# Filter spectrum stored on SP's queue from the first step of u on, two more input chunks in the positions' space, first spilled reads on SP

## The chip, the cores and the metric

One Trainium2 chip, one of its cores. The metric is the device time of one execution in microseconds (us); of several runs the median is given, and less is better.

## The reference, cut to what matters

```python
h_mlp = np.maximum(pos_emb @ w1, 0.0) @ w2          # [12480, 128], the filter
h_filt = h_mlp * np.exp(-0.01 * pos)[:, None]
u = x * v
y = irfft(rfft(u, 2 * S) * rfft(h_filt, 2 * S))[:S]  # causal long convolution
x1 = x * y
...
h = x1 @ w_in;  x2 = np.maximum(h, 0.0) ** 2 @ w_out              # first MLP, 128 -> 2048 -> 128
h = x2 @ w_in2; out = (h * sigmoid(1.702 * h)) @ w_out2           # second MLP
```

## The kernel before

The convolution is done as a two-step Fourier transform with 99 x 127 points, in matmuls. The program falls into these stages on the time line.

1. **Filter stage** (`filter_stage`). 16 transfers bring the positions' embeddings `pos`; matmuls, a relu and a window make `h`, 64 features, in SBUF. On the way the loads of the first chunks of `x` and `v` are issued.
2. **First transform of h.** 16 calls of `s1_step`, each 4 features: 8 matmuls (two records each in the trace) into a PSUM bank, then one copy on ACT into `G`, the filter's spectrum after the first step. Four PSUM banks rotate.
3. **First transform of u.** 32 calls of `s1_step`, each 4 of the 128 channels, into `A`. Their input is `u = x * v`, folded by VectorE (`Inputs.fold`: one multiplication, L206, then a sum, L207, and a difference, L208). `x` and `v` come in 16 chunks of 8 channels; a chunk feeds two steps. `Inputs.load` issues a chunk as four transfers on SP's queue: 96 rows of `x`, 96 rows of `v`, then the last 3 rows of each. `u` has 7 buffers.
4. **Second transform, product, first inverse** (`stage_s2`), with matrices `m` loaded on SP's queue and slices `Gs` of the filter's spectrum.
5. **Inverse and the two MLPs** (`mlp`).

`G` and `A` do not both fit for all of stage 4, so `G` is spilled: in stage 3 four transfers store it to `gd` in device memory (L637, ACT's queue, after steps 6, 10, 14 and 18 of u), and `load_h` reads it back in slices of 8 (`Gs`, L278, ACT's queue; the first two are issued after steps 26 and 28 of u).

Where chunks live: the first 5 have a buffer each beside `h` (pool `hp`). All others share 3 buffers in pool `vp`, so chunk 8 waits until chunk 5 is folded, chunk 9 until chunk 6 is folded, and so on. The code lines are

```python
c = self.loaded
if c == NXC or c >= self.early and c - max(self.done, self.early) == 3:
    return
```

`mh`, the pool of `w2b`, `m` and `Gs`, is opened after the last chunk's load is issued and lies where `vp` lay; a tile of it waits for the chunks whose bytes it takes. `A` lies where `hp` lay.

The order of the instructions on each engine is that of the code (`manual_schedule`). An engine's queue issues in order: a transfer that waits holds back what stands behind it, and on ACT's queue transfers stand between the copies. Each transfer signals its end on one of eight semaphores, which the built program hands out in turn over both queues; a transfer waits until the transfer before it on its semaphore has landed.

Of the kernel before, what the change touches and what calls it, by code (L numbers as in the profile page):

```python
# [23 lines left out]
N1, N2 = 99, 127  # L24
# [4 lines left out]
F = 64  # L29
# [5 lines left out]
NXC = D // XC  # L35
HK = 4
HL = 8
# [54 lines left out]
def conv_mlp_kernel(ctx: ExitStack, tc: tile.TileContext, xc, xt, vc, pt, w1, w2,  # L92
                    moe_w_in, moe_w_out, moe2_w_in, moe2_w_out,
                    c_s1, c_s2, c_i2, c_win, out):
    nc = tc.nc
# [8 lines left out]
    gd = dram.tile([128, N1, 2 * F], FP32, name="gd")  # L104
# [45 lines left out]
    def split_weights(pool, l):  # L150
        wr = pool.tile([128, 4 * DFF], FP32, name=f"w{l}").bitcast(F32R)
        wr = wr.rearrange("p (a b) -> p a b", a=4)
        wts.append(wr)

    class Weights:
# [3 lines left out]
        def __init__(self, chunks, start, gap, lead, pool, rest=()):  # L159
            self.pool, self.raw, self.run = pool, {}, []  # L160
            self.plan = [(int(start + k * gap), n) for k, n in enumerate(chunks)]
            self.fetches = [(at - lead, n) for at, n in self.plan] + [(at, n) for at, n in rest]
            self.plan += [(1 << 30, n) for at, n in rest]
# [15 lines left out]
    class Inputs:  # L179


        def __init__(self, up, pool, first, early):
            self.up, self.pool, self.tiles, self.u = up, pool, {}, {}
            self.first, self.early = first, early
            self.loaded = self.done = 0

        def load(self):
            c = self.loaded
            if c == NXC or c >= self.early and c - max(self.done, self.early) == 3:
                return  # L190
            self.loaded += 1
            pool, bufs = (self.first, self.early) if c < self.early else (self.pool, 3)
            xs, vs = (pool.tile([N1, XC, 2, NJ], FP32, tag=n, name=n, bufs=bufs) for n in ("x", "v"))
            for r in (slice(0, ROWS), slice(ROWS, N1)):
                nc.sync.dma_start(out=xs[r], in_=xc[c, r])
                nc.sync.dma_start(out=vs[r], in_=vc[c, r])
            self.tiles[c] = xs, vs
# [56 lines left out]
    def s1_step(bank, src, d, dst):  # L254


        ps = bank("s1").rearrange("p (e k) -> p e k", e=4)[:, :, 0:2 * N1]
        for e in range(4):
            for half in range(2):
                j = slice(half * NJ, (half + 1) * NJ)  # L260
                nc.tensor.matmul(out=ps[j, e], lhsT=src[:, d + e, j], rhs=cs1[:, half])  # L261
        nc.scalar.copy(out=dst, in_=ps.rearrange("p e (c k) -> p k c e", c=2))

    m_t, h_t = {}, {}

    def load_m(mp, p):
        if p >= NP:
            return
        n = min(2, N1 - 2 * p)
        m_t[p] = mp.tile([128, 2, 2, 128], FP32, tag="m", name="m", bufs=7)  # L270
        nc.sync.dma_start(out=m_t[p][:, 0:n], in_=c_s2[:, 2 * p:2 * p + n])

    def load_h(mp, g):
        if g >= NHL:
            return
        n = min(HL, N1 - g * HL)
        h_t[g] = mp.tile([128, HL, 2 * F], FP32, tag="Gs", name="Gs", bufs=2)
        nc.scalar.dma_start(out=h_t[g][:, 0:n], in_=gd[:, g * HL:g * HL + n])  # L278

    def stage_s2(sp, mp, A, w2b, hooks, work):  # L280

# [8 lines left out]
        with kp as kp, obp as obp:  # L290
# [57 lines left out]
            for p in range(NP + 2):  # L348
                if p < NP:
                    spectra(p)  # L350
                if p % 2 == 0:
                    features(p // 2 + 1)
                if 0 <= p - 2:
                    back(p - 2)
                load_m(mp, p + 5)
                if p % 4 == 1:
                    load_h(mp, p // 4 + 2)
                if 0 <= p - 1 < NP:
                    product(p - 1)
                work.tick(p)  # L360
                for f in hooks.get(p, ()):
                    f()
# [18 lines left out]
    def load_x(lp, t):  # L381
        x_t[t] = lp.tile([D, MW], FP32, tag="xs", name="xs", bufs=2)
        w = width(t)
        nc.sync.dma_start(out=x_t[t][:, 0:w], in_=xt[:, STARTS[t]:STARTS[t] + w])
# [214 lines left out]
    with tc.manual_schedule():  # L599
        ups, sgs, vps = ExitStack(), ExitStack(), ExitStack()  # L600
        up = ups.enter_context(tc.tile_pool(name="u", bufs=7, side="right", reuse_waits="tile"))
        cps = ups.enter_context(tc.tile_pool(name="bank", bufs=4, space=PSUM))

        def bank(name):
            return cps.tile([128, 1024], FP32, tag="b", name=name)

        G = sgs.enter_context(tc.tile_pool(name="G", bufs=1, side="right")).tile(
            [128, N1, 2, F], FP32, name="G")
        vp = vps.enter_context(tc.tile_pool(name="v", bufs=3, side="right"))
        folds = {max(-(-11 * c // 5) + 1, 2 * c + 4 if c >= 7 else 0) for c in range(NXC)}  # L610
        steps = [0]

        def advance():
            if steps[0] in folds:
                inputs.fold()
            inputs.load()
            steps[0] += 1

        with tc.tile_pool(name="h", bufs=1) as hp:
            h = hp.tile([N1, F, 2 * NJ], FP32, name="h")  # L620
            inputs = Inputs(up, vp, hp, 5)
            with tc.tile_pool(name="fil", bufs=2) as fp:
                filter_stage(fp, bank, h, inputs)
            for f in range(0, F, 4):
                s1_step(bank, h, f, G[:, :, :, f:f + 4])
                advance()
            assert inputs.done >= inputs.early
        with tc.tile_pool(name="A", bufs=1, reuse_waits="tile") as ap_, ExitStack() as mps:
            A = ap_.tile([128, N1, 2, D], FP32, name="A")
            for d in range(0, D, 4):  # L630
                s1_step(bank, inputs.u[d // XC], d % XC, A[:, :, :, d:d + 4])
                if d // 4 < 22:
                    advance()
                if d // 4 in (6, 10, 14, 18):
                    q = 25 * (d // 16 - 1)
                    q = slice(q, min(q + 25, N1))
                    nc.scalar.dma_start(out=gd[:, q], in_=G[:, q].rearrange("p k c f -> p k (c f)"))  # L637
                if d // 4 == 22:
                    assert inputs.done == NXC
                    vps.close()  # L640
                    mp = mps.enter_context(tc.tile_pool(name="mh", bufs=1, reuse_waits="tile"))
                    w2b = mp.tile([128, 2 * D], FP32, name="w2b")
                    nc.sync.dma_start(out=w2b, in_=w2)
                if 22 <= d // 4 < 27:
                    load_m(mp, d // 4 - 22)
                if d // 4 in (26, 28):
                    load_h(mp, (d // 4 - 26) // 2)
            sgs.close()
            ups.close()
            w0 = ctx.enter_context(tc.tile_pool(name="w0", bufs=1, side="right", reuse_waits="tile"))  # L650
            split_weights(w0, 0)
            cp = ctx.enter_context(tc.tile_pool(name="cvt", bufs=1, side="right", reuse_waits="tile"))
            lp = ctx.enter_context(tc.tile_pool(name="lp", bufs=2, side="right", reuse_waits="tile"))
            nc.sync.dma_start(out=ci2, in_=c_i2)
            work = Weights([0, 4, 1, 5, 2, 6], 3, 7, 5, cp, [(44, 3), (46, 7)])
            hooks = {44: [lambda: load_x(lp, 0)]}
            with tc.tile_pool(name="s2", bufs=1, side="right", reuse_waits="tile") as sp:
                stage_s2(sp, mp, A, w2b, hooks, work)
        w1_ = ctx.enter_context(tc.tile_pool(name="w1", bufs=1, side="right", reuse_waits="tile"))
        split_weights(w1_, 1)  # L660
        mlp(lp, cp)
# [89 lines left out]
```

## Time and profile before

| what | value |
|---|---|
| median of 3 runs | 1435.65 us (1435.14 to 1436.28) |
| profiled execution, its own time | 1431.45 us |
| its span, first to last instruction | 1429.7 us |
| mean granted TensorE clock in it | 0.992 |
| PE busy, share of the span | 98% |
| DVE, ACT, POOL busy | 78%, 66%, 16% |

A busy share is the time in which an engine had an instruction under way; a waiting PE shows as a gap, a throttled one as a granted clock under 1. The median is of runs without a profile.

### The profile page before, as it was taken

Reading aid. Unit: us, or ns where it says so; the run is one execution under the profiler, and the core shown is the slowest. Engines: PE = TensorE matmul, PEld = TensorE weight load, DVE = VectorE, ACT = ScalarE, POOL = GpSimd, SP = SyncE. Lnnn points to the kernel's source line nnn. Section 1 sums busy time; section 2 is a strip of 40 time slices with the busy share of each in tenths; the row PEclk is TensorE's granted clock in tenths of the full one; section 3 lists DMA queues with packets and bytes.
Section 4 is the critical chain, followed back from the end, with each engine's and each line's share of the span. In section 5 each row is a group of like instructions: output and inputs, shape, how many; then the busy total and the mean of one; then the engine's idle time right before and its main releaser. Section 6 shows DMA issues by size and latency. Waiting matters only on the chain.

```text
span 1429.7 us, 17766 instructions
## 1 busy us (share of the span) xinstructions
PE 1403.7 (98%) x7018; PEld 1177.1 (82%) x7018; DVE 1115.9 (78%) x1233; ACT 939.9 (66%) x1066; POOL 224.8 (16%) x209
## 2 busy tenths in 40 slices
PE   8989999999999999999999999999999999999998
PEld 7858888688878888888888888888888888888887
DVE  7348998699997777877778777877777777777887
ACT  2534454377767776776777777776777776777776
POOL 3002232317521110021101210112101120000000
PEclk9989999899999999999999999999999999999999
DMA  9586766411300001000001000010000000000000
GB/s 254 198 264 216 250 230 224 154 44 64 96 6 22 19 27 38 8 26 19 27 9 36 19 27 26 8 38 19 26 11 24 30 26 8 8 8 1 15 15 15
DMA packets 46400, 91.34 MB, mean 64 GB/s; under 512 B 4183, under 2 KB 30604, under 8 KB 45804
## 3 DMA queue, kind: packets, MB, share of 16 engines
q1 hardware_dynamic: 35886, 57.17, 13.8%
q10 hardware_dynamic: 10430, 33.03, 6.0%
q8 instruction: 55, 0.90, 0.3%
q14 instruction: 29, 0.24, 0.0%
HBM read 64.33 MB, written 25.85 MB: 63 GB/s over the span
## 4 chain that ended last, share of the span: by engine, by line
PE 92%; DVE 4%; DMA 3%; ACT 1%; issue 1%; SPq 0%; DVEq 0%; ACTq 0%
PE hin L484 12%; PE hin L483 12%; PE acc L484 12%; PE hin L485 12%; PE acc L483 12%; PE acc L485 12%; PE yps L441 4%; PE s L261 3%; PE hk L311 3%; PE xk L313 3%; PE ob L337 3%; PE fk L300 2%; DMA v<-in_vc_dram 1%; DVE gl L521 1%; DMA gd<-G 1%; DVE r L245 1%
## 5 line engine op out<-in xcount | busy, mean ns | idle before, releaser
L521 DVE TENSOR_TENSOR gl<-g,gh 128x1004 fp32r<-128x1004 f32 (+4 forms) x400 | 491.1, 1228 | 35.7 <-ACT gh L517 35.4
L501 ACT ACTIVATE g<-hin 128x1004 f32<-128x1004 f32 (+4 forms) x200 | 201.2, 1006 | 231.5 <-PE hin L485 231.1
L484 PE MATMUL acc<-gl,w 128*128 128x502 f32 (+4 forms) x800 | 311.6, 390 | 3.1 <-DVE gl L521 3.1
L483 PE MATMUL acc<-gh,w 128*128 128x502 f32 (+4 forms) x800 | 313.0, 391 | 0.6 <-DVE lo L430 0.6
L483 PE MATMUL hin<-hi,w 128*128 128x502 f32 (+4 forms) x800 | 312.5, 391 | 0.0
L484 PE MATMUL hin<-lo,w 128*128 128x502 f32 (+4 forms) x800 | 312.1, 390 | 0.0
L485 PE MATMUL hin<-hi,w 128*128 128x502 f32 (+4 forms) x800 | 311.5, 389 | 0.0
L485 PE MATMUL acc<-gh,w 128*128 128x502 f32 (+4 forms) x800 | 311.2, 389 | 0.0
L512 DVE TENSOR_TENSOR g<-hin,g 128x1004 f32<-128x1004 f32 (+4 forms) x200 | 238.5, 1193 | 50.7 <-ACT g L504 50.6
L388 POOL TENSOR_TENSOR b<-uv 99x256 f32<-99x256 f32 x127 | 160.9, 1297 | 696.6 <-DMA uv<-bd 538.7
L510 DVE CAST gh<-g 128x1004 fp32r<-128x1004 f32 (+4 forms) x200 | 142.7, 713 | 145.1 <-ACT g L502 144.9
L504 ACT ACTIVATE g<-hin 128x1004 f32<-128x1004 f32 (+4 forms) x200 | 200.1, 1000 | 75.2 <-PE hin L485 67.3
L502 ACT ACTIVATE g<-g 128x1004 f32<-128x1004 f32 (+4 forms) x200 | 208.0, 1040 | 6.3
L517 ACT CAST gh<-g 128x1004 fp32r<-128x1004 f32 (+4 forms) x200 | 202.7, 1014 | 0.3 <-DVE g L512 0.3
L484 PEld LDWEIGHTS acc<-gl,w 128*128 128x128 f32 x800 | 150.8, 188 | 34.8 <-DVE gl L521 5.0
L483 PEld LDWEIGHTS hin<-hi,w 128*128 128x128 f32 x800 | 151.1, 189 | 34.0 <-ACT g L501 2.4
L485 PEld LDWEIGHTS hin<-hi,w 128*128 128x128 f32 x800 | 151.2, 189 | 30.7
L483 PEld LDWEIGHTS acc<-gh,w 128*128 128x128 f32 x800 | 150.8, 189 | 31.0 <-DVE lo L430 1.0
L484 PEld LDWEIGHTS hin<-lo,w 128*128 128x128 f32 x800 | 151.1, 189 | 30.4 <-DVE lo L430 0.5
L485 PEld LDWEIGHTS acc<-gh,w 128*128 128x128 f32 x800 | 150.5, 188 | 30.2
L324 DVE TENSOR_TENSOR t<-xk,hc 128x512 f32<-128x512 f32 (+1 forms) x100 | 63.7, 678 | 26.0 <-PE xk L313 20.7
L328 POOL TENSOR_TENSOR P<-t,t 128x256 f32<-128x256 f32 (+1 forms) x50 | 43.8, 876 | 191.4 <-DVE t L324 95.0
(56 smaller groups left out, 1043.2 us busy)
## 6 DMA issues: line engine op xcount, KB each, us to landing
uv<-bd SPq DMA_DIRECT2D x64, 198.0 KB
m<-in_c_s_dram SPq DMA_DIRECT2D x49, 256.0 KB
bd<-bs ACTq DMA_DIRECT2D x24, 512.0 KB
x<-in_xc_dram SPq DMA_DIRECT2D x16, 384.0 KB
v<-in_vc_dram SPq DMA_DIRECT2D x16, 384.0 KB
Gs<-gd ACTq DMA_DIRECT2D x12, 512.0 KB
gd<-G ACTq DMA_DIRECT2D x3, 1600.0 KB
raw<-in_moe_w_in_dram SPq DMA_DIRECT2D x8, 512.0 KB
```

Of the source, the lines that this page charges most:

```text
L324: nc.vector.tensor_tensor(out=t[c][:, 0:n], in0=xk[:, 0:n, c].unsqueeze(2).to_broadcast([128, n, 2, D]), in1=hc[:, 0:n], op=ALU.mult)
L388: engine.tensor_tensor(out=b[:, :, s, c], in0=uv[:, 0, :, c], in1=uv[:, 1, :, 1 - c], op=ALU.add if s != c else ALU.subtract)
L483: nc.tensor.matmul(out=out, lhsT=a, rhs=hl[0], start=first, stop=False)
L484: nc.tensor.matmul(out=out, lhsT=a, rhs=hl[1], start=False, stop=False)
L485: nc.tensor.matmul(out=out, lhsT=b, rhs=hl[0], start=False, stop=last)
L501: nc.scalar.activation(out=g, in_=ps, func=ACTF.Relu)
L502: nc.scalar.activation(out=g, in_=g, func=ACTF.Square)
L504: nc.scalar.activation(out=g, in_=ps, func=ACTF.Sigmoid, scale=1.702)
L510: nc.vector.tensor_copy(out=gh, in_=g)
L512: nc.vector.tensor_tensor(out=g, in0=ps, in1=g, op=ALU.mult)
L517: nc.scalar.copy(out=gh, in_=g)
L521: nc.vector.tensor_tensor(out=gl, in0=g, in1=gh.bitcast(FP32), op=ALU.subtract)
```

## The change

It does five things.

- Three kinds of homes for the chunks: 5 in `hp` as before, then 2 in a new pool `h2`, which takes the space that the filter stage's pool (positions, window, `r`) leaves when it closes, then 3 in `vp`. So chunks 5 to 9 are issued with no wait for a fold, and chunk 10 is the first that waits for one, that of chunk 7. Loads of chunks 5 and 6 come after the filter stage in the program instead of in it.
- The four stores of `G` go from ACT's queue to SP's.
- They stand after steps 0, 3, 6 and 9 of u instead of 6, 10, 14 and 18, and ahead of the chunk that the same step issues.
- The first two reads of `Gs` go from ACT's queue to SP's.
- They stand after steps 23 and 25 instead of 26 and 28, behind the `m` load of the same step. Later `Gs` reads stay on ACT's queue.

Nothing that is computed, and no transfer's size, changes.

```diff
+        def home(self, pool, bufs):
+            self.homes.append((len(self.homes) and sum(h[2] for h in self.homes), pool, bufs))
         def load(self):
             c = self.loaded
-            if c == NXC or c >= self.early and c - max(self.done, self.early) == 3:
+            if c == NXC:
+                return
+            start, pool, bufs = [h for h in self.homes if h[0] <= c][-1]
+            if c - max(self.done, start) >= bufs:
                 return
             self.loaded += 1
-            pool, bufs = (self.first, self.early) if c < self.early else (self.pool, 3)
...
-    def load_h(mp, g):
+    def load_h(mp, g, queue=nc.scalar):
...
-        nc.scalar.dma_start(out=h_t[g][:, 0:n], in_=gd[:, g * HL:g * HL + n])
+        queue.dma_start(out=h_t[g][:, 0:n], in_=gd[:, g * HL:g * HL + n])
...
-            inputs = Inputs(up, vp, hp, 5)
+            inputs = Inputs(up)
+            inputs.home(hp, 5)
             with tc.tile_pool(name="fil", bufs=2) as fp:
                 filter_stage(fp, bank, h, inputs)
-            for f in range(0, F, 4):
-                s1_step(bank, h, f, G[:, :, :, f:f + 4])
-                advance()
-            assert inputs.done >= inputs.early
+            with tc.tile_pool(name="h2", bufs=1, reuse_waits="tile") as hp2:
+                inputs.home(hp2, 2)
+                inputs.home(vp, 3)
+                for f in range(0, F, 4):
+                    s1_step(bank, h, f, G[:, :, :, f:f + 4])
+                    advance()
+                assert inputs.done >= 7
...
                 s1_step(bank, inputs.u[d // XC], d % XC, A[:, :, :, d:d + 4])
+                if d // 4 in (0, 3, 6, 9):
+                    q = 25 * (d // 12)
+                    q = slice(q, min(q + 25, N1))
+                    nc.sync.dma_start(out=gd[:, q], in_=G[:, q].rearrange("p k c f -> p k (c f)"))
                 if d // 4 < 22:
                     advance()
-                if d // 4 in (6, 10, 14, 18):
-                    q = 25 * (d // 16 - 1)
-                    q = slice(q, min(q + 25, N1))
-                    nc.scalar.dma_start(out=gd[:, q], in_=G[:, q].rearrange("p k c f -> p k (c f)"))
...
-                if d // 4 in (26, 28):
-                    load_h(mp, (d // 4 - 26) // 2)
+                if d // 4 in (23, 25):
+                    load_h(mp, (d // 4 - 23) // 2, nc.sync)
```

SP's queue in the middle of the loads, before: the last transfers of chunk 8 (`x_441`, `v_442`), then chunk 9 (`x_481`, `v_482`), then the head of chunk 10 (`x_526`).

```order
L195 DMA x_441<-in_xc_dram 3x1024
L196 DMA v_442<-in_vc_dram 3x1024
L195 DMA x_481<-in_xc_dram 96x1024
L196 DMA v_482<-in_vc_dram 96x1024
L195 DMA x_481<-in_xc_dram 3x1024
L196 DMA v_482<-in_vc_dram 3x1024
L195 DMA x_526<-in_xc_dram 96x1024
```

The same place of SP's queue now (lines stand 5 lower): the last of chunk 9 (`x_354`, `v_355`), the first store, chunk 10 (`x_531`, `v_532`), the second store, the head of chunk 11, and so on to chunk 12; then chunk 13, the fourth store, chunks 14 and 15.

```order
L200 DMA x_354<-in_xc_dram 3x1024
L201 DMA v_355<-in_vc_dram 3x1024
L644 DMA gd_63<-G_75 128x3200
L200 DMA x_531<-in_xc_dram 96x1024
L201 DMA v_532<-in_vc_dram 96x1024
L200 DMA x_531<-in_xc_dram 3x1024
L201 DMA v_532<-in_vc_dram 3x1024
L644 DMA gd_63<-G_75 128x3200
L200 DMA x_562<-in_xc_dram 96x1024
```

The first store now stands behind chunk 9 instead of on ACT, where seven copies into `A` stood ahead of it. The first reads of `Gs` on ACT's queue before, among the last copies into `A`:

```order
L262 COPY A<-s_842 128x198x4
L278 DMA Gs<-gd 128x1024
L262 COPY A<-s_856 128x198x4
L262 COPY A<-s_866 128x198x4
L278 DMA Gs<-gd 128x1024
L262 COPY A<-s_878 128x198x4
L262 COPY A<-s_888 128x198x4
L262 COPY A<-s_898 128x198x4
L303 COPY fs<-fk 128x512
```

The same reads on SP's queue now, among the loads of `m`, right behind the last chunk:

```order
L652 DMA w2b<-in_w_dram 128x256
L276 DMA m<-in_c_s_dram 128x512 x2
L283 DMA Gs<-gd 128x1024
L276 DMA m<-in_c_s_dram 128x512 x2
L283 DMA Gs<-gd 128x1024
L276 DMA m<-in_c_s_dram 128x512
```

No copy into `A` now stands behind a read of `Gs`; the third, fourth and fifth `m` stand behind one instead.

## Rows read from the trace of the kernel before

**Rows 1.** The page: engines' busy time and share, and the chain that ended last.

```profile
PE 1403.7 (98%) x7018; PEld 1177.1 (82%) x7018; DVE 1115.9 (78%) x1233; ACT 939.9 (66%) x1066; POOL 224.8 (16%) x209
...
PE 92%; DVE 4%; DMA 3%; ACT 1%; issue 1%; SPq 0%; DVEq 0%; ACTq 0%
```

**Rows 2.** By stretch: sum; PE, PEld, DVE, ACT, POOL busy; clock, DMA share, GB/s.

```profile
69.80:105.00 35.20, 27.57 (x225) 20.06 (x225) 17.62 (x21) 11.89 (x15) 0.00 (x0) 0.85 0.84 262
105.00:249.00 144.00, 142.07 (x749) 127.37 (x750) 122.12 (x185) 70.12 (x121) 40.72 (x46) 1.00 0.69 232
```

**Rows 3.** Timeline of PE: start, length, instruction; idle time before it, releaser.

```profile
45.22 0.33 PE L261 MATMUL s<-cs,u 99*64 99x198 f32 x1
...
72.45 5.09 PE L261 MATMUL s<-cs,u 99*64 99x198 f32 x32 [2.62 <-DVE u L207]
...
105.00 1.13 PE L300 MATMUL fk<-m,Gs 128*128 128x128 f32 x8 [1.59 <-DMA Gs<-gd]
...
108.64 1.05 PE L300 MATMUL fk<-m,Gs 128*128 128x128 f32 x8
```

**Rows 4.** What SP's queue waited for, 40 to 105 us: total, times, longest.

```profile
SPq L195 <- DMA gd<-G: 26.3, 3, 18.0
SPq L196 <- DMA gd<-G: 5.2, 1, 5.2
```

**Rows 5.** Timeline of SP's queue; issue time, then how long the issue took.

```profile
42.16 0.25 SPq L196 DMA_DIRECT2D v<-in_vc_dram  x1
60.49 0.32 SPq L195 DMA_DIRECT2D x<-in_xc_dram  x1
...
84.09 0.32 SPq L195 DMA_DIRECT2D x<-in_xc_dram  x1
```

**Rows 6.** Timeline of ACT and its queue.

```profile
45.75 0.82 ACT L262 COPY G<-s 128x792 f32<-128x792 f32 x1 [0.52 <-PE s L261]
...
49.77 0.82 ACT L262 COPY A<-s 128x792 f32<-128x792 f32 x1 [0.52 <-PE s L261]
51.11 0.82 ACT L262 COPY A<-s 128x792 f32<-128x792 f32 x1 [0.52 <-PE s L261]
...
55.19 0.36 ACTq L637 DMA_DIRECT2D gd<-G  x1
```

**Rows 7.** Timeline of DVE's folds.

```profile
49.04 0.68 DVE L208 TENSOR_TENSOR u<-x 99x512 f32<-99x512 f32 x1
...
70.29 1.22 DVE L206 TENSOR_TENSOR x<-x,v 99x1024 f32<-99x1024 f32 x1 [17.88 <-DMA v<-in_vc_dram]
71.62 0.69 DVE L207 TENSOR_TENSOR u<-x 99x512 f32<-99x512 f32 x1
...
90.44 1.23 DVE L206 TENSOR_TENSOR x<-x,v 99x1024 f32<-99x1024 f32 x1 [1.40 <-DMA v<-in_vc_dram]
```

**Rows 8.** By stretch again, for the transfers: columns as in Rows 2.

```profile
24.00:36.00 12.00, 12.00 (x143) 10.28 (x144) 11.83 (x16) 6.55 (x8) 0.00 (x0) 1.00 1.03 241
44.00:56.00 12.00, 12.00 (x148) 10.31 (x146) 3.98 (x6) 7.37 (x9) 0.00 (x0) 1.00 0.02 7
56.00:60.00 4.00, 4.00 (x52) 3.44 (x50) 0.00 (x0) 2.45 (x3) 0.00 (x0) 1.00 0.98 410
```

**Rows 9.** The page's issues of transfers: times issued, size.

```profile
x<-in_xc_dram SPq DMA_DIRECT2D x16, 384.0 KB
v<-in_vc_dram SPq DMA_DIRECT2D x16, 384.0 KB
...
gd<-G ACTq DMA_DIRECT2D x3, 1600.0 KB
```

**Rows 10.** The chain that ended last, in order of time: start, length, what.

```profile
91.00 6.72 DMA v<-in_vc_dram
...
97.84 1.23 DVE x L206
...
100.50 4.37 DMA Gs<-gd
```

More of the change, by code (lines that the diff above doesn't have):

```diff
@@ L179, in conv_mlp_kernel, with __init__ @@
     class Inputs:
-        def __init__(self, up, pool, first, early):
-            self.up, self.pool, self.tiles, self.u = up, pool, {}, {}
-            self.first, self.early = first, early
+        def __init__(self, up):
+            self.up, self.tiles, self.u, self.homes = up, {}, {}, []
             self.loaded = self.done = 0
+        def home(self, pool, bufs):
+            self.homes.append((len(self.homes) and sum(h[2] for h in self.homes), pool, bufs))
         def load(self):
             c = self.loaded
-            if c == NXC or c >= self.early and c - max(self.done, self.early) == 3:
+            if c == NXC:
+                return
+            start, pool, bufs = [h for h in self.homes if h[0] <= c][-1]
+            if c - max(self.done, start) >= bufs:
                 return
             self.loaded += 1
-            pool, bufs = (self.first, self.early) if c < self.early else (self.pool, 3)
             xs, vs = (pool.tile([N1, XC, 2, NJ], FP32, tag=n, name=n, bufs=bufs) for n in ("x", "v"))
```

## The prediction

> **What bounds the kernel now.** I read the page first. PE is busy for 98% of the span and makes up 92% of the chain that ended last [rows 1]. So time can only come from the places where PE stands or crawls, and the question is where the change's stage has such a place. The view by stretch answers it: from 105 to 249 us PE lacks 1.93 us of 144, but from 69.80 to 105.00 it is busy for 27.57 of 35.20 us, at a granted clock of 0.85 [rows 2]. That stretch is the second half of the transform of u. Its matmuls need far less: a step takes 1.34 us, the distance of two copies into A (49.77 and 51.11) [rows 6].
>
> PE's timeline shows the ends of the stage: u's first step starts at 45.22, the second transform (fk) at 105.00, released by the read of Gs [rows 3]. 32 steps of 1.34 us from 45.22 end at 88.1. **So 16.9 us of this stage are waiting**, and that is the most that the stage can give.
>
> What is waited for? DVE's fold of chunk 9 stands for 17.88 us until 70.29, for a transfer of v [rows 7]. SP's queue names the cause: it waits 26.3 us in three waits, the longest 18.0, and 5.2 in another, for stores of G [rows 4]. Chunk 9 issues at 60.49, though the transfer before it was issued at 42.16 [rows 5]; the store that it waited for left ACT at 55.19, behind seven copies into A [rows 6]. From 44 to 56 the transfer engines are busy for 2% [rows 8]. From then on chunks come late, one after the other, to the end of the chain: v's last wait 6.72, the fold of chunk 15 at 97.84, then the read of Gs, 4.37 [rows 10].
>
> **The change, part by part.**
>
> *Store out of ACT's order.* G is complete at 46.57, the end of its last copy (45.75 + 0.82) [rows 6]; the first store can be issued then instead of at 55.19. SP holds it there, and behind it on SP only chunk 10 waits, which must anyway wait for the fold of chunk 7, done at 49.72 (49.04 + 0.68) [rows 7]. So this wait costs nothing. ACT loses six transfers from among its copies; its time there is not on the path.
>
> *Two more homes.* Chunks 8 and 9 no longer wait for a fold or for a store. Chunk 8's bytes are through at about 44 [rows 8], and chunk 9 follows at once.
>
> *The stream from then on.* A chunk is 2 x (384 + 12) KB = 811 kB (12 KB is three rows of 4 KB) and a store 1638 kB, the last 1573 kB (24 slices instead of 25) [rows 9]. Loads alone on SP's queue run at 241 GB/s with full engines (24 to 36 us), stores alone at 410 GB/s (56 to 60 us) [rows 8]: 3.37 us a chunk, 4.0 a store (3.84 the last). Both lists now stand in one queue, in the order s 10 s 11 s 12 13 s 14 15. Each transfer waits for one that stands eight places before it, about two chunks, so I take them as back to back: chunk 9 ends at 44 + 3.4 = 47.4, then 6 x 3.37 + 15.8 = 36.0, and chunk 15's bytes end at 83.4. From issue of the first store to the wait that it ends is 60.49 - 55.19 = 5.3 [rows 5, 6], of which 4.0 are bytes; of the 1.3 left I put half behind the last byte. Chunk 15 has landed at 84.05.
>
> *To the last step.* From the fold's start to PE's first matmul on it is 72.45 - 70.29 = 2.16 [rows 3, 7], so PE gets chunk 15 at 86.2. It would want it at 45.22 + 30 x 1.34 = 85.4. It waits 0.8 and ends its two steps at 88.9. Chunk 14 lands 3.4 earlier, 80.65, in time for 82.7.
>
> *The reads of Gs.* They stand behind the second m load, which takes bytes of chunk 14's home. Its fold ends at about 80.65 + 1.22 + 0.69 + 0.68 = 83.2 [rows 7]; m and Gs are issued by 83.6, and with 4.37 [rows 10] Gs lands at 88.0, under the cover of the last two steps. If that cover were gone, it would cost what it is late, 4.4 at most. The third and fourth m wait for the fold of chunk 15, 86.6, and feed the second fk group, 3.6 us behind the first (108.64 - 105.00) [rows 3], so at 92.5: again 4.4 is enough, by 1.1 us.
>
> **The sum.** fk starts at 88.9 instead of 105.0: 16.1 us less. Behind it nothing depends on a time of day: PE is full from there on, so I carry the gain to the end. Against the profiled execution's 1431.45 (span 1429.7) this is 1415.35; the median of the runs shown is 4.2 us above it, and I take the difference as it is: 1435.65 - 16.1 = 1419.55, **1419.5 us**.
>
> **A rule that speaks against it.** The rows show load after load at full engines with no gap (share 1.03) [rows 8], so a transfer's own start and end are hidden as long as others are in flight. The Trainium skill, page "DMA: Bandwidth & Descriptors", section "Anatomy of one DMA", gives each DMA a fixed part of about 2.0 us beside its bytes, most of it the receipt of the write. By that, paid by each of the ten transfers, chunk 15 would land some 20 us later than I say, and the change would lose. The store of before, 5.3 us for 4.0 us of bytes, agrees with a fixed part (1.3 here); whether it is paid ten times is the rivals' question.
>
> **The rivals.**
>
> *A. Gaps or slow stores.* At each of the eight changes between a store and a chunk the 1.3 us show, or stores run at the loads' 241 GB/s in the shared queue: 8 x 1.3 = 10.4, or 15.8 x (410/241 - 1) = 11.1. Gain 5 to 5.7, so 1430. For it: no row shows the two kinds in one queue. Against it: the eight semaphores let two chunks be under way, and in all of 24 to 36 us no gap shows. Half of it, 1425.
>
> *B. Not the transfers, but PE itself.* All lands a little sooner, since loads between stores run faster than 241. Then PE is the bound, the gain is 16.9, and with what is missing from 105 to 249 us [rows 2] at most 18.8: 1418.7 to 1416.8. If the 4.2 us by which the median is above the profile lie in the transfers of before, up to 1415. This is the same mechanism as the forecast's, with another last step.
>
> *C. The start of the second transform starves.* m and Gs now compete behind chunk 15 with nothing loaded ahead; the second fk group comes 1.1 us after my estimate of its m. If they are 3 us later, 2 us are given back: 1421.5.
>
> *D. Slower.* Each store and each chunk is issued only when the one before it has landed: the last small loads of a chunk wait for a store's semaphore, and SP stands in order. A store takes 5.3; a chunk by itself, from issue to fold, 90.44 - 84.09 = 6.35 [rows 5, 7]. From 46.57 this is 4 x 5.3 + 6 x 6.35 = 59.3: chunk 15 at 105.9 instead of the 97.84 at which its fold starts now [rows 10]. 8 us worse, 1443.7. It decides from 51.3 us for the ten on (97.84 - 46.57), 5.1 each, where back to back is 3.6.
>
> *E. It doesn't do what it says.* The engines are full from 56 us on anyway, and the bytes are the same, so earlier stores only push loads back. Against it: 12 us of idle engines from 44 to 56 [rows 8] are there to be filled, and E would need all of them to come back as waits elsewhere: 1435 or so.
>
> **How the numbers follow.** Forecast with B and C, gain 13.5 to 18.8 (up to 20 in the runs): 0.76. A, or half of it, gain 4 to 13.5: 0.17. E: 0.04. D: 0.03. A change under 0.2%, 2.9 us, is about what a measurement of this kernel can't tell from none. So faster 0.93, same 0.04, slower 0.03. Of the forecast's part I leave out the last 0.05 below 1416.0, and of A's the upper half, above 1426: with D and E that is less than 0.2. Range 1416.0 to 1426.0.
>
> **What would show it.** First store issued on SP at about 46.6; engines busy for over 90% from 47 to 83 us; fold of chunk 10 at about 55.5, of chunk 15 at 84; PE's waits in the stage under 2 us, its granted clock 1.00; fk at 88 to 90. I am wrong if SP still waits for stores while the engines are idle, if the fold of chunk 15 starts after 90, or if fk starts early and the stage from there to the MLPs is longer than the 144 us of now.

## The result and the profile after

| | before | after |
|---|---|---|
| median of four runs | 1435.97 us | 1418.91 us (1415.44 to 1420.76) |
| profiled execution: own time, span | 1431.45, 1429.7 us | 1419.01, 1417.2 us |

The ratio of the times is 0.9879, with a 95% interval of 0.986 to 0.9898: 17.1 us less, and at least 14.6. The time is the predicted one to 0.6 us. The profiled execution of the changed kernel is one of its four runs; that of the kernel before is not among its four. One run of a kernel below, e9_stores_late, took 6355 us and is left out of its numbers.

The page's first rows of the changed kernel, engines and chain [rows 1]:

```profile
PE 1399.3 (99%) x7018; PEld 1175.7 (83%) x7018; DVE 1114.3 (79%) x1233; ACT 940.4 (66%) x1066; POOL 221.2 (16%) x209
...
PE 92%; DVE 4%; issue 1%; DMA 1%; ACT 1%; POOL 0%; SPq 0%; DVEq 0%; POOLq 0%; ACTq 0%
```

The transfers' 3% of the chain have become 1%. SP's queue, the stores (L644), chunk 10 (51.12) and the first read of `Gs` [rows 5]:

```profile
47.96 0.36 SPq L644 DMA_DIRECT2D gd<-G  x1
51.12 0.32 SPq L200 DMA_DIRECT2D x<-in_xc_dram  x1
...
52.94 0.35 SPq L644 DMA_DIRECT2D gd<-G  x1
...
57.83 0.35 SPq L644 DMA_DIRECT2D gd<-G  x1
...
69.79 0.35 SPq L644 DMA_DIRECT2D gd<-G  x1
...
85.20 0.43 SPq L283 DMA_DIRECT2D Gs<-gd  x1
```

What SP's queue waited for from 40 to 105 us (total, times, longest), where before stood three waits of 26.3 us in all and one of 5.2 [rows 4]:

```profile
SPq L201 <- DMA gd<-G: 5.4, 2, 3.2
...
SPq L200 <- DMA gd<-G: 2.0, 1, 2.0
```

The windows of the stage [rows 2, 8], then DVE's folds of chunks 10 and 15 [rows 7], then PE [rows 3]:

```profile
47.90:84.00 36.10, 36.10 (x436) 30.81 (x431) 17.86 (x22) 22.02 (x28) 0.00 (x0) 1.00 0.97 327
84.00:90.00 6.00, 6.00 (x68) 4.62 (x65) 3.32 (x5) 3.27 (x5) 0.00 (x0) 1.00 0.65 201
```

```profile
57.67 1.22 DVE L211 TENSOR_TENSOR x<-x,v 99x1024 f32<-99x1024 f32 x1 [1.22 <-DMA v<-in_vc_dram]
...
85.02 1.23 DVE L211 TENSOR_TENSOR x<-x,v 99x1024 f32<-99x1024 f32 x1 [0.22 <-DMA v<-in_vc_dram]
```

```profile
46.58 0.33 PE L266 MATMUL s<-cs,u 99*64 99x198 f32 x1
...
46.75 43.85 PE L266 MATMUL s<-cs,u 99*64 99x198 f32 x511
90.53 1.16 PE L305 MATMUL fk<-m,Gs 128*128 128x128 f32 x8
```

From the first store to 84 us the transfer engines are full (0.97). PE's rows show the 512 records of the stage without a break, and fk behind them with no wait: 90.53 instead of 105.00. One small wait hides in that long row. ACT's copies into `A`, one for each step, come 1.34 us apart in this kernel too, but for two near the end:

```profile
84.63 0.82 ACT L267 COPY A<-s 128x792 f32<-128x792 f32 x1 [0.52 <-PE s L266]
86.45 0.82 ACT L267 COPY A<-s 128x792 f32<-128x792 f32 x1 [1.00 <-PE s L266]
87.79 0.82 ACT L267 COPY A<-s 128x792 f32<-128x792 f32 x1 [0.52 <-PE s L266]
89.29 0.82 ACT L267 COPY A<-s 128x792 f32<-128x792 f32 x1 [0.69 <-PE s L266]
```

The copy of chunk 14's first step comes 0.48 us late (86.45 - 84.63 is 1.82), that of chunk 15's first step 0.16: the loads still hold PE for 0.64 us. The length of the stage, from u's first step to fk, is 43.95 us instead of 59.78.

### The profile page after: what moved, and what is told of

The parts are those of the page before. It is cut to its first block, busy times and chain, and to the rows that moved or that the text cites. A ratio compares the mean times of both kernels' runs of the same rounds, so it can differ in the third digit from the quotient of the medians.

```text
span 1417.2 us, 17764 instructions
## 1 busy us (share of the span) xinstructions
PE 1399.3 (99%) x7018; PEld 1175.7 (83%) x7018; DVE 1114.3 (79%) x1233; ACT 940.4 (66%) x1066; POOL 221.2 (16%) x209
## 4 chain that ended last, share of the span: by engine, by line
PE 92%; DVE 4%; issue 1%; DMA 1%; ACT 1%; POOL 0%; SPq 0%; DVEq 0%; POOLq 0%; ACTq 0%
PE hin L489 12%; PE hin L490 12%; PE hin L488 12%; PE acc L489 12%; PE acc L488 12%; PE acc L490 12%; PE s L266 5%; PE yps L446 4%; PE hk L316 3%; PE xk L318 3%; PE ob L342 3%; PE fk L305 2%; DVE gl L526 1%; DVE r L250 1%; DMA uv<-bd 1%
```

## The experiments

In each group of kernels below, the runs of the kernel before on the same chip gave its own median; the difference is to that. The ratio is an estimate over all runs and the difference one of two medians; they disagree by up to 1.4 us (e1: 18.0 and 19.4).

| label | stores of G: queue, steps | further homes | first Gs reads | ratio, 95% interval | difference, us | fk in the profile |
|---|---|---|---|---|---|---|
| (before) | ACT, late | no | ACT | | | 105.00 |
| (after) | SP, early | yes | SP | 0.9879 (0.986 to 0.9898) | -17.1 | 90.53 |
| e1_stores_sp | SP, early | no | ACT | 0.9875 (0.9846 to 0.9905) | -19.4 | 90.44 |
| e2_homes_only | ACT, late | yes | ACT | 0.9923 (0.9904 to 0.9941) | -11.0 | 97.83 |
| e3_stores_act | ACT, early | yes | SP | 0.9876 (0.9854 to 0.9898) | -16.9 | 92.26 |
| e5_gs_only | ACT, late | no | SP | 1.0006 (0.9989 to 1.0023) | +0.9 | 107.00 |
| e6_stores_early_act | ACT, early | no | ACT | 0.9976 (0.9966 to 0.9987) | -3.8 | 101.79 |
| e7_one_more_store | SP, early, 5 stores | yes | SP | 0.9922 (0.9902 to 0.9942) | -10.8 | 98.21 |
| e8_two_more_stores | SP, early, 6 stores | yes | SP | 0.9944 (0.9922 to 0.9965) | -7.3 | 101.24 |
| e9_stores_late | ACT, after steps 18 to 21 | no | ACT | 1.0012 (0.9992 to 1.0031) | +1.8 | 108.41 |
| e10_queue_only | SP, late | no | ACT | 0.9884 (0.9858 to 0.991) | -15.3 | 91.12 |
| e11_after_old_steps | SP, late | yes | SP | 0.9892 (0.9874 to 0.991) | -15.9 | 89.93 |
| e12_after_again | as after | yes | SP | 0.9894 (0.988 to 0.9909) | -15.4 | 90.34 |

"Late" is after steps 6, 10, 14, 18 of u, "early" after 0, 3, 6, 9. The theory at the start was that of the prediction: SP stands on a store that leaves ACT late, and the transfers of the stage then run back to back. The rivals were that the homes, or the reads of `Gs`, carry the gain, and that PE or the transfers have slack left.

### The parts by themselves

The stores alone, on the kernel before:

```diff
+                if d // 4 in (0, 3, 6, 9):
+                    q = 25 * (d // 12)
+                    q = slice(q, min(q + 25, N1))
+                    nc.sync.dma_start(out=gd[:, q], in_=G[:, q].rearrange("p k c f -> p k (c f)"))
                 if d // 4 < 22:
                     advance()
-                if d // 4 in (6, 10, 14, 18):
-                    q = 25 * (d // 16 - 1)
...
-                    nc.scalar.dma_start(out=gd[:, q], in_=G[:, q].rearrange("p k c f -> p k (c f)"))
```

> The kernel before with one part of the change: the four stores of G on SP's queue after steps 0, 3, 6 and 9 of u; homes of the chunks and reads of Gs as before. Theory (the stores held back by ACT's order, and what stands on their semaphores, were the whole stall): nearly all of the change's gain, 14 to 17 us less than before; second transform starts at 90 to 92 us, at most 1.5 later than in the changed kernel, because Gs on ACT's queue waits for the fold of chunk 15. Rival (the two homes carry it: chunk 9 waits for a fold): under 8 us less, chunk 9 issued late.

It is as fast as the changed kernel, and 13.7 to 22.1 us below the kernel before by its interval: the stores carry the whole gain. Its PE rows:

```profile
45.40 43.41 PE L261 MATMUL s<-cs,u 99*64 99x198 f32 x511
90.44 1.13 PE L300 MATMUL fk<-m,Gs 128*128 128x128 f32 x8 [1.63 <-DMA Gs<-gd]
```

The only wait left is 1.63 us for the first `Gs`, which the changed kernel hides; in the times of the runs no trace of it is to be seen.

The homes alone are the changed kernel with the stores and the reads of `Gs` as before (its diff is that of the change, backwards, in these two places).

> The kernel before with one part of the change: the two more homes; stores on ACT's queue after steps 6, 10, 14 and 18, Gs on ACT's queue, as before. Theory of the stores: chunk 10's last rows stand on the first store's semaphore in the built program, so SP stands until about 60.5 us again, one chunk further on; five chunks and three stores are left then, 29 us, chunk 15 lands at about 89, second transform at about 94: 9 to 12 us less than before. Rival of the homes: 14 us less or more.

The gain is 11.0 us, as the theory of the stores had it, though fk comes 3.8 us later than it said (97.83). SP's waits show what the homes do and what they can't:

```profile
SPq L200 <- DMA gd<-G: 15.0, 3, 9.9
...
SPq L201 <- DMA gd<-G: 4.5, 1, 4.5
```

The stand on the first store is still there, but it comes one chunk later: chunk 9 leaves at 42.81, and the last rows of chunk 10 wait from 51.7 to 61.58. The gains of homes and stores overlap; they don't add up.

The reads of `Gs` alone:

```diff
-                if d // 4 in (26, 28):
-                    load_h(mp, (d // 4 - 26) // 2)
+                if d // 4 in (23, 25):
+                    load_h(mp, (d // 4 - 23) // 2, nc.sync)
```

> The kernel before with one part of the change: the first two reads of Gs on SP's queue after steps 23 and 25. Theory: they wait for the fold of chunk 15 behind the second m in any case, so second transform within 1.5 us of 105, time within 2 us of before. Rival (ACT's copies behind the reads were on the path): 3 us less or more.

No difference: the reads wait for chunk 15's home either way, and SP still stands for 20.5 us on a store.

### Queue or time?

Is it that the store leaves earlier, or that it is in SP's queue? First the changed kernel with its early stores on ACT:

```diff
-                    nc.sync.dma_start(out=gd[:, q], in_=G[:, q].rearrange("p k c f -> p k (c f)"))
+                    nc.scalar.dma_start(out=gd[:, q], in_=G[:, q].rearrange("p k c f -> p k (c f)"))
```

> The changed kernel with the four stores on ACT's queue at the same early steps (0, 3, 6, 9). If only the time of the store counts: same as the changed kernel within 1.5 us. Theory (a store on another queue also holds SP through the semaphores, and shares the engines packet by packet with x and v): store issued behind the first copy into A at 48, chunk 9 stands on it and waits until about 53 instead of 42, engines idle for 4 to 5 us more: second transform 2 to 6 us later than in the changed kernel, 12 to 15 us less than before.

The times can't be told from the changed kernel's, so of the two readings the first held, and the theory's 12 to 15 us and 2 to 6 us at fk were too pessimistic: the profile has fk 1.7 us later. SP stands all the same:

```profile
SPq L200 <- DMA gd<-G: 13.5, 2, 11.6
```

Chunk 9's last rows stand on the first store until 54.10. So with two homes more the kernel carries a stand of 11.6 us. Now the same early steps on ACT in the kernel before (the diff as in the first experiment, with `nc.scalar` for `nc.sync`).

> The kernel before, with its four stores still on ACT's queue, but after steps 0, 3, 6 and 9 of u. Nothing else of the change. Theory (what costs is that SP stands on the semaphore of the first store, and so the time at which that store lands): the store leaves ACT at about 47 to 48 instead of 55.2 and lands some 5.3 us later, at 53; chunk 9 is issued at 53 instead of 60.5, and the second transform starts 7 to 12 us earlier, so 1425 to 1430 against a before of 1437. Rival (the queue is what matters, since SP's order alone keeps the loads fed): no more than 3 us less, 1434 or above. Rival (time of the stores is all that matters): as with the stores on SP, 17 to 20 us less, 1417 to 1420.

The gain is 3.8 us, and fk comes 3.2 us earlier (101.79), where the theory had 7 to 12. ACT's queue, SP's queue and SP's waits tell why:

```profile
48.24 0.36 ACTq L635 DMA_DIRECT2D gd<-G  x1
```

```profile
53.78 0.25 SPq L196 DMA_DIRECT2D v<-in_vc_dram  x1
```

```profile
SPq L196 <- DMA gd<-G: 18.6, 2, 16.5
```

The store leaves 7 us earlier than before [rows 6], as was meant. But with the stores elsewhere in the code another load stands on the first one: the last rows of chunk 7, which wait 16.5 us. SP is free 6.7 us earlier than before (60.49 [rows 5]), but with a chunk more to load; and PE, which has fewer waits in the stage, then waits 3.81 us for `Gs` ahead of fk.

Next, stores later than before, behind the last load in the code:

```diff
-                if d // 4 in (6, 10, 14, 18):
-                    q = 25 * (d // 16 - 1)
+                if d // 4 in (18, 19, 20, 21):
+                    q = 25 * (d // 4 - 18)
```

> The kernel before, with its stores still on ACT's queue but later than before, after steps 18 to 21 of u: in the program's order they come behind the last load of x and v, so that no load can stand on a store's semaphore. Theory (not the lateness of a store, but a load that stands on it, costs): SP waits for no store while chunks are loaded, PE waits for nothing until its last steps; the stores leave at 69 to 74, their bytes end at 86 to 88, and the second transform starts at 89 to 94: 10 to 16 us less than before, 1421 to 1427 against 1437. Rival (stores must be early, since the transfers as a whole are the bound): slower than before, 1440 or more.

The expectation was wrong: no gain. The assumption that the semaphores follow the order of the code was wrong. SP's longest single stand in all these kernels is on a store that the code issues behind the load:

```profile
SPq L195 <- DMA gd<-G: 22.6, 1, 22.6
```

```profile
56.86 0.43 SPq L196 DMA_DIRECT2D v<-in_vc_dram  x1
79.93 0.25 SPq L195 DMA_DIRECT2D x<-in_xc_dram  x1
```

```profile
72.65 0.36 ACTq L637 DMA_DIRECT2D gd<-G  x1
```

```profile
57.00:73.00 16.00, 16.00 (x194) 13.72 (x192) 4.71 (x6) 9.74 (x13) 0.00 (x0) 1.00 0.29 71
```

The last three rows of chunk 12 (12 KB) wait for a store that ACT, busy with copies, issues at 72.65; the transfer engines are at 0.29 for 16 us. In the built program the store signals its end on semaphore DMAHW7, and the last `x` rows of chunk 12 are the next transfer on it and wait for it (ACT's queue, then SP's; the store itself waits for an earlier transfer on it):

```
41 L637 DMA gd<-G 128x3200 [waits DMAHW7_49,Activation_49]
...
63 L195 DMA x<-in_xc_dram 3x1024 [waits DMAHW7_49]
```

No data passes between them. That is the mechanism of the kernel before in pure form: there the head of chunk 9 is the next transfer behind the first store on their semaphore.

Then the decisive one: the kernel before with one word changed, all steps as they were.

```diff
-                    nc.scalar.dma_start(out=gd[:, q], in_=G[:, q].rearrange("p k c f -> p k (c f)"))
+                    nc.sync.dma_start(out=gd[:, q], in_=G[:, q].rearrange("p k c f -> p k (c f)"))
```

> The kernel before with one word changed: its four stores of G on SP's queue, in the old places of the program (after steps 6, 10, 14 and 18 of u). On SP that is behind chunk 12, behind chunk 14, and twice behind chunk 15. Theory as it stands after the run with early stores on ACT (what costs is a load that stands on a store in the other queue, which leaves late; a store in SP's own order is never waited for before it has left): SP waits for no store for more than 3 us; the engines idle some 5 us up to 51, where chunk 9 waits for the fold of chunk 6; from there seven chunks and four stores end at about 90, chunk 15 well before, so the second transform starts at 91 to 95 and the time is 10 to 16 us less than before, 1421 to 1427. Rival (early steps are what counts): as the early stores on ACT, 3 to 5 us less. Rival (the queue alone gives it all): 17 to 20 less.

1419.36 us, 15.3 less, where the changed kernel itself gave 15.4 on the same chip (e12): the whole gain. It lies in the theory's 10 to 16 us, as fk at 91.12 does in its 91 to 95; its interval, 13 to 20 us, doesn't exclude the last rival's 17 to 20. The expectation had the wait for a fold one chunk too early: it is chunk 10 that waits, at 51.06, for chunk 7. SP, DVE (fold of chunk 15) and PE:

```profile
59.07 0.36 SPq L637 DMA_DIRECT2D gd<-G  x1
```

```profile
79.83 1.22 DVE L206 TENSOR_TENSOR x<-x,v 99x1024 f32<-99x1024 f32 x1 [3.73 <-DMA v<-in_vc_dram]
```

```profile
46.70 43.20 PE L261 MATMUL s<-cs,u 99*64 99x198 f32 x511
91.12 1.13 PE L300 MATMUL fk<-m,Gs 128*128 128x128 f32 x8 [1.23 <-DMA Gs<-gd]
```

The first store leaves at 59.07, **3.9 us later than before** (55.19 [rows 6]), and yet fk starts 13.9 us earlier. An early store isn't needed. What the one word takes away is the load that stands on a store which another engine issues late. SP's longest wait for a store up to 80 us is 2.3 here. With the late steps chunk 15 even comes 5.2 us sooner than in the changed kernel (79.83 for 85.02), since two stores now follow it instead of preceding it. The changed kernel with the late steps, its stores again behind the chunk of the same step, shows the same:

```diff
-                if d // 4 in (0, 3, 6, 9):
-                    q = 25 * (d // 12)
...
+                if d // 4 in (6, 10, 14, 18):
+                    q = 25 * (d // 16 - 1)
```

> The changed kernel with its stores on SP's queue, but after steps 6, 10, 14 and 18 again. Theory: all is in one queue and the two further homes fill the engines up to 51, so that the same bytes end at 84 to 86 with chunk 15 ahead of the last two stores; PE is the bound, and the time is that of the changed kernel within 2 us. Rival (the last stores now hold back m and Gs): 3 to 8 us more than the changed kernel.

1418.73 us, the changed kernel's time, with fk at 89.93 after a wait of 0.23 us for `Gs`. The copies into `A` come 1.34 us apart to the last in both kernels with late stores on SP: there PE is the bound of the stage, and neither homes, nor steps, nor the queue of `Gs` can be seen in the times.

### How much slack is left

A further store of the same size to a scratch that nobody reads, behind the second one (in the second kernel behind the third one too, with `(3, 6)` for `(3,)`):

```diff
+    ge = dram.tile([128, 2, 25, 2 * F], FP32, name="ge")
...
-                    nc.sync.dma_start(out=gd[:, q], in_=G[:, q].rearrange("p k c f -> p k (c f)"))
+                    src = G[:, q].rearrange("p k c f -> p k (c f)")
+                    nc.sync.dma_start(out=gd[:, q], in_=src)
+                    if d // 4 in (3,):
+                        nc.sync.dma_start(out=ge[:, d // 4 // 3 - 1], in_=src)
```

> The changed kernel with one more store of 1600 KB behind the second one, to a scratch that nobody reads. Theory (from 47 to 84 us the transfers run back to back, and chunk 15 comes just as PE wants it: fold at 85.0, wanted at 84.8): each further store delays chunk 15 by its bytes, 4.0 us at 410 GB/s, and the second transform with it: 3.5 to 4.5 us more than the changed kernel. Rival (PE is the bound, with spare time in the transfers): 0 to 1 us more. Rival (each store costs a start and an end of its own): 5.3 us or more.

> As the run before, with a further store of 1600 KB behind the third one too. Theory (back to back, no slack): 7.5 to 9 us more than the changed kernel, twice the run before. Rival (spare time in the transfers): less than 5 us. Rival (5.3 us or more for each): 10.5 us or more.

Against the two ratios of the changed kernel (0.9879 and 0.9894) these are 4.0 to 6.2 us and 7.2 to 9.3 us more: transfers without slack. DVE's fold of chunk 15 in the one and in the other:

```profile
90.72 1.23 DVE L212 TENSOR_TENSOR x<-x,v 99x1024 f32<-99x1024 f32 x1 [0.27 <-DMA v<-in_vc_dram]
```

```profile
94.24 1.23 DVE L212 TENSOR_TENSOR x<-x,v 99x1024 f32<-99x1024 f32 x1 [0.24 <-DMA v<-in_vc_dram]
```

Counted from u's first step (46.58, 48.53, 48.71) the fold comes at 38.4, 42.2 and 45.5: 3.8 and 3.3 us for a store, no more than its 4.0 us of bytes [rows 8]. What the first one costs beyond that is PE's clock. PE waited 3.50 us for chunk 14, the granted clock fell in that wait to 0.50 of 2.4 GHz, and the four steps behind it took 8.28 us instead of 4 x 1.34 = 5.4. This window of the kernel with one more store shows the clock:

```profile
88.20:95.00 6.80, 5.00 (x30) 4.78 (x32) 4.67 (x6) 0.82 (x1) 0.00 (x0) 0.50 0.61 192
```

The Trainium skill, page "DMA: Bandwidth & Descriptors", section "Anatomy of one DMA — SWDGE (gpsimd) path", has a fixed part of about 2.0 us for each DMA beside its bytes. The section is on the DMAs that GpSimd issues; SP issues these stores. For a further store in this full queue the runs show no such part (3.8 and 3.3 us for 4.0 of bytes). The prediction charged it to ten transfers; with four to a chunk they were 28.

### The profile's missing 4.6 us

The profiled executions differ by 12.4 us (1431.45 and 1419.01), the medians by 17.1. The changed kernel once more, unchanged:

> The changed kernel once more, unchanged. Theory (the stretches at the half clock at 25 and at 370 us in its first profile come by chance, not with the change): its profile has the second transform at 88 to 91, no fixed pattern of half-clock stretches at those places, and its time is 1415 to 1421. Rival (they belong to the change): the same two stretches again, and a span within 0.5 us of 1417.2.

The theory fell: the same two stretches come again, and the span is 1417.3. The windows of before, of the changed kernel and of its second profile (the third last column is the granted clock):

```profile
23.50:45.00 21.50, 21.45 (x252) 18.22 (x254) 18.91 (x23) 12.05 (x15) 0.00 (x0) 1.00 0.91 220
```

```profile
23.50:45.00 21.50, 21.50 (x236) 17.73 (x236) 18.37 (x23) 11.21 (x14) 0.00 (x0) 0.92 0.97 239
...
360.00:400.00 40.00, 37.94 (x161) 31.06 (x160) 34.38 (x46) 25.40 (x28) 17.82 (x14) 0.91 0.17 58
```

```profile
360.00:400.00 40.00, 38.00 (x161) 31.07 (x160) 33.78 (x45) 25.44 (x28) 17.84 (x14) 0.91 0.19 58
```

The first stretch, in the transform of h, is not the change's doing: it stands in eleven of the thirteen profiles, those of the kernels with the code of before in this place among them (0.92 in the two with stores late or early on ACT). Only the profile of before and that of e1 were without it. It comes behind a wait of PE for the last of `h`, which all thirteen have; of before, then of the changed kernel:

```profile
23.55 22.00 PE L261 MATMUL s<-cs,h 99*64 99x198 f32 x255 [3.27 <-DVE h L249]
```

```profile
23.23 23.68 PE L266 MATMUL s<-cs,h 99*64 99x198 f32 x255 [3.34 <-DVE h L254]
```

So about the same wait was followed by 2.4 GHz in two profiles and by 1.2 in eleven. In the changed kernel this makes u start 1.4 us later, so 1.4 of the 4.6 us are a difference between two executions. The second stretch, in the inverse, where PE of the changed kernel waited for POOL three times just before (1.7 us in all), stands in five of the thirteen; why there is open. From fk to the end the thirteen profiles take 1323.9 to 1329.4 us, the kernel before 1324.7, the changed one 1326.7 and 1327.0. One profile of each kernel can't tell such differences from the change, and the rest of the 4.6 us stays open.

## Why the prediction was right, and where its reasons were not

- **What bounds.** Right. The 16.9 us of waiting were the place: the stage is 15.8 us shorter, and 1.1 us remain above 32 x 1.34, 0.64 of them the wait for chunks 14 and 15.
- **First store at 46.57.** It came at 47.96; the 1.4 us are u's later first step (46.58 instead of 45.22), from the half clock in the transform of h.
- **The stream, 36.0 us.** It took 36.4 (47.96 to 85.02, less 0.65 for the end), at 0.97 of the engines. The two averages of before, 241 and 410 GB/s, add up in the mixed queue.
- **The last step.** I had PE wait 0.8 us, for chunk 15, and took chunk 14 to be in time. PE waited 0.64 us, 0.48 of them for chunk 14, whose fold starts at 82.18; with the prediction's 2.16 us that is 84.34, and PE wanted it at 46.58 + 28 x 1.34 = 84.10. So the transfers, not PE, still set the last steps, as forecast, and rival B's last step is not what happened. The margin is nil: a further store costs its bytes.
- **The reads of Gs.** Issued at 85.20 instead of 83.6, and under cover, as said.
- **"PE is full from there on, so I carry the gain to the end."** Not quite in the profile: from fk to the end it is 1326.7 us for 1324.7 before. The 15.8 us of the stage are 14.5 at fk, since u starts 1.4 later, and 12.5 at the end; in the medians it is 17.1 for the 16.1 of the sum. The stage confirms the mechanism; that the time came out to 0.6 us is in part luck, since 4.6 us between profiles and medians are only accounted for to 1.4.
- **Rivals.** A (gaps at each change between store and chunk) and D (one after the other) are out by the further stores; C by fk with no wait and its second group 3.66 us behind the first (94.19), as before; E by the time.
- **What was wrong is a part of the cause.** I priced the store as one that leaves 8.6 us earlier, with two homes to fill the hole. The store in SP's queue at the old steps leaves later than before and gains as much; the same early steps on ACT gain 3.8 us. The step "the store that it waited for left ACT at 55.19" was right as a reading, but I took the lateness for the fault, and the fault was the stand of one queue on the other's semaphore. The homes are worth 11 us alone and nothing measurable beside the queue; the `Gs` reads nothing in either.

## What to carry to other kernels

When a queue of loads waits for a transfer with which it shares no data, ask which semaphore the two share and who issues the other one; a transfer that an engine issues between its own work, late, held every load behind it here, even where only 12 KB stood on it. Put such a transfer into the queue that would have to wait for it: there it leaves in order, and a single word did here what five edits were made for. Test the edits one at a time, since two that fill the same hole each look needed.

## What the runs showed of the hardware

- Stores and loads in one queue from SP keep the transfer engines full: 327 GB/s at a share of 0.97 over 36 us, and in the kernel with one word changed, where three stores come close together and two reads of `Gs` on ACT's queue follow, this from 70 to 90 us:

```profile
70.00:90.00 20.00, 19.90 (x236) 16.81 (x232) 7.46 (x9) 12.18 (x16) 0.00 (x0) 1.00 1.01 395
```

- PE's clock fell from 2.4 to 1.2 GHz in a wait of 3.50 us, so that the wait cost more than its length: in the kernel with one more store fk is 5.7 us later, counted from u's first step, for chunks that are 3.7 and 3.8 us late. In the kernel with two more stores two shorter waits, 2.20 and 2.27 us, also had it at 0.50 a few us later (86 to 88 and 96 to 98 us).
